# Half-sequence layout, larger moved pieces, loads issued from GpSimd and a check in tiles of its own, in a gated linear attention with a Switch expert layer

## The chip, the cores and the metric

The kernel runs on one core of a Trainium2 chip. The metric is the device time of one execution in microseconds (us); lower is better. Engines are named as in the profile: PE (matrix products), DVE (vector engine), ACT (activation functions), POOL (GpSimd), SP (the sync engine, which issues DMAs). L363 is line 363 of the kernel.

## The reference

Attention has 4 batches of 8 heads, 768 positions and 48 elements a head; the expert layer has 8 experts of 1,024 hidden elements, one for each token.

```python
mag = np.sqrt(a_re * a_re + a_im * a_im)
scale = np.minimum(mag, 0.999) / (mag + 1e-06)
a_re_n, a_im_n = (a_re * scale, a_im * scale)
for t in range(S):
    ar, ai = (a_re_n[:, :, t, :, None], a_im_n[:, :, t, :, None])
    new_re = ar * S_re - ai * S_im
    new_im = ar * S_im + ai * S_re
    kv = np.einsum('bhd,bhe->bhde', k[:, :, t], v[:, :, t])
    S_re, S_im = (new_re + kv, new_im)
    y[:, :, t] = np.einsum('bhd,bhde->bhe', q[:, :, t], S_re)
...
# x = y as (3072, 384)
logits = x @ w_gate
expert_idx = np.argmax(logits, axis=1)
# probs = softmax of logits, gate_w = probs of the chosen expert
for e in range(E):
    xe = x[expert_idx == e]
    out[expert_idx == e] = gate_w[...] * (np.maximum(xe @ w1[e], 0.0) @ w2[e])
```

## The kernel before

The recurrence is rewritten: the products of the gates up to a position become a sum of logarithms and a sum of angles, queries and keys are scaled and rotated by them, and what is left is a causal linear attention in chunks of 128 positions with a state carried between chunks.

**Units and the front.** The 3,072 positions are cut into ten units: 128, 256 and 384 positions of batch 0, two of 384 in batches 1 and 2, then 384, 256 and 128 in batch 3. `front(u)` loads a unit's gates into tile `AB` and its queries and keys into `Z` (`ld`, L280, on SP's queue; 128 partitions, two arrays, three groups of heads G, up to TU = 384 positions in fp32). ACT takes Ln and Exp, POOL multiplies `im` by the inverse, DVE works through L291 (square, whose largest value goes to `chk`), L295, L299 and the three scans of L301 (sum of logarithms), then a product of the keys, the scans of L312 (sum of angles) and L317 to L320 (whole turns off), ACT takes sine and cosine, and four products on DVE (in line 170, a helper that all products share) write the rotated keys and queries to `zp`. There are two tiles each of `AB`, `Z` and `C`, and one each of `D`, `cs` and `zp`.

**Moves.** In `zp` 128 partitions hold head elements in three groups; PE wants each head's real and imaginary parts in 96 partitions. Ten DMAs per unit (L333), five blocks for each of the two parts, move `zp` to a slot of `hz`, from SBUF to SBUF. The blocks hold three, two or one heads. Both tiles are stored by 128 positions, so that the longest piece that one DMA descriptor moves is 3 heads x 128 positions x 4 bytes = 1,536 bytes.

**Chunks.** `chunk(b, c)` works through 128 positions on PE: it turns the keys (L363, copied by ACT, L365), takes scores of four heads into a bank (L370), which DVE masks into `am` (line 170, `am<-bank,causal`), multiplies the carried state (L382) and the masked scores (L389) with queries and values, brings the state forward (L397), and turns the result into rows of tokens with the logits of the experts (L405; L411 sums the logits). `load_v` (L342) loads values by half sequences into three tiles. `route` finds each token's expert and place, and POOL scatters rows to the buffer `xs_hbm`, one DMA for 128 tokens (L467). Three DMAs (L495) fill rows of the buffer that no token may reach.

**The order of the work.** Nothing above is issued as it stands in the text. Each call adds an operation to a `Plan`, with its engine, an assumed duration, its reads and writes and, for a DMA, its size. `P.order()` simulates this list, takes the best of several orders, and the kernel writes each engine's instructions in that order; the hardware keeps it on every engine and waits on semaphores. `RATE` is the assumed rate of a DMA; one clock `dma` holds for all queues together. `after=` makes an operation start after others have been issued. Loads of unit u are placed behind the moves of unit u-2:

```python
P.add("SP", 0.65, lambda: nc.sync.dma_start(o[:, :, :, sl], src[b, :, :, :, t0:t1]), (), keys, lat=1.5, kb=2 * n * 0.512, after=moved[u - 2] if u > 1 else ())
```

**The check and the experts.** After the attention a few small DVE instructions and two matmuls (L511 to L536) find whether a general path is needed; its flag, `again`, is read later and the general path, a loop at the end, is not entered on these inputs. The check's tiles come from a pool of their own, `chkp`, opened after the attention's pool has closed; then the pool of the experts is opened. A second plan orders the experts: SP loads weights `w1b` (L573) and `w2b` (L575) and rows `xr` (L576, L579); PE turns the rows (L587) and does the two products (L598, L612; L627 for the ends of two experts together); ACT and DVE apply relu and the gate (L604, L601, L567); POOL scatters to the output (L556).

Of the kernel before, what the change touches and what calls it, by code (L numbers as in the profile page):

```python
# [43 lines left out]
class Plan:  # L44
# [25 lines left out]

    XL, TBL, RATE, SLACK = 0.12, 1.3, 0.30, 0.05

# [19 lines left out]
    def run(self, prio, edges, ins, back, stick):  # L92


        ops, n = self.ops, [len(x) for x in ins]
        ready, start = [0.0] * len(ops), [0.0] * len(ops)
        cur, dma, per_kb = None, 0.0, 1 / self.RATE / 1e3
        port, other = {"DVE": 0.0, "POOL": 0.0}, {"DVE": "POOL", "POOL": "DVE"}
        free, cand = {o["eng"]: 0.0 for o in ops}, {o["eng"]: [] for o in ops}
        for o in ops:  # L100
            if n[o["i"]] == 0:
                cand[o["eng"]].append(o["i"])
        for _ in ops:
            pick = None
            for eng, cs in cand.items():
                if not cs:
                    continue
                f = free[eng]
                fp = max(f, port[other[eng]]) if eng in port else f
                at = [max(fp if ops[i]["port"] else f, ready[i]) for i in cs]  # L110
                low = min(at)
                if pick is not None and low >= pick[2]:
                    continue
                best = None
                for i, t in zip(cs, at):
# [41 lines left out]
def gateloop_then_moe(ctx, tc, gates, qk, v, wg, w1, w2, out):  # L157
# [57 lines left out]
    with ExitStack() as att:  # L215
# [44 lines left out]
        moved = {}  # L260

        def front(u):
            b, t0, t1 = UNITS[u]
# [60 lines left out]
            for part, key, tr in ((1, Sk, si), (0, ("co",), co)):  # L324
                for x, xk, src in ((1, K, kk), (0, Q, qq)):
                    P.add("DVE", dve2(n), lambda part=part, tr=tr, x=x, src=src: tt(
                        zp[:, part, 0:nch, x].rearrange("p c g t -> p g c t"), src.rearrange("p g (c t) -> p g c t", t=128),
                        tr.rearrange("p g (c t) -> p g c t", t=128), ALU.mult), (xk,) + tuple(key), (("zp", part, x),), port=True)
            for part in (1, 0):
                for p0, p1, g0, g1, h0, d0 in BLOCKS:  # L330
                    m, r0 = g1 - g0, part * D + d0
                    eng, dma = ("ACT", nc.scalar) if u == 0 and part == 0 and h0 else ("SP", nc.sync)
                    i = P.add(eng, 0.65, lambda dma=dma, p0=p0, p1=p1, g0=g0, g1=g1, h0=h0, r0=r0, m=m, part=part: dma.dma_start(  # L333
                        hz[slot][r0:r0 + p1 - p0, cl:cl + nch, :, h0:h0 + m].rearrange("p c x h t -> p (c x) h t"),
                        zp[p0:p1, part, 0:nch, :, g0:g1].rearrange("p c x g t -> p (c x) g t")),
                        (("zp", part, 0), ("zp", part, 1)), tuple(("h", slot, cl + x, h, part, d0) for x in range(nch) for h in range(h0, h0 + m)),
                        lat=1.6, kb=2 * (p1 - p0) * m * T * 4 / 1e3)
                    moved.setdefault(u, []).append(i)

        def load_v(b, half):  # L340
            i = 2 * b + half
            P.add("SP", 0.08, lambda: nc.sync.dma_start(  # L342
                vb[i % 3], v[b, 3 * half:3 * half + 3].rearrange("c p f -> p c f")), (), (("v", i % 3),), lat=1.9, kb=590, after=moved.get(2 * b + half - 1, ()))

        def chunk(b, c):
            i = 2 * b + c // 3
# [5 lines left out]

            hq, hk = hz[slot][:, cl, 0], hz[slot][:, cl, 1]

# [132 lines left out]
        with tc.manual_schedule():  # L487
            for u in range(NU):
# [4 lines left out]
                if u == 3:  # L493
                    for h in range(3):
                        P.add("SP", 0.65, lambda h=h: nc.sync.dma_start(  # L495
                            xs_hbm.rearrange("(e s) w -> s e w", e=E)[MINC + 64 * h:MINC + 64 * h + 64],
                            bc(empty[0:64, None, :], [64, E, W])), (), (("empty", h),), lat=2, kb=E * 64 * W * 4 / 1e3, after=moved[1])
                for c in range(t0 // 128, t1 // 128):
                    chunk(b, c)
                    for r0, r1 in ROUTES[b]:  # L500
# [10 lines left out]
    again = consts.tile([1, 1], I32, name="again")  # L511
    with ExitStack() as fs:
        fp = fs.enter_context(tc.tile_pool(name="chkp", bufs=1, reuse_waits="tile"))
        ok = fp.tile([128, 4], FP32, name="ok")
        f1 = fp.tile([128, NU], FP32, name="f1")
        nc.vector.tensor_scalar(out=f1, in0=chk, scalar1=2.25, scalar2=None, op0=ALU.is_le)
        nc.vector.tensor_reduce(ok[:, 0:1], f1, axis=AX, op=ALU.min)
        lv = lend.rearrange("p b g c -> p (b g) c")
        f2 = fp.tile([128, B * G, C], FP32, name="f2")
        tt(f2, lv[:, :, 1:], lv[:, :, :C], ALU.subtract)  # L520
        nc.vector.tensor_scalar(out=f2, in0=f2, scalar1=-60.0, scalar2=None, op0=ALU.is_ge)
        nc.vector.tensor_reduce(ok[:, 1:2], f2.rearrange("p a c -> p (a c)"), axis=AX, op=ALU.min)
        f3 = fp.tile([128, B * G], FP32, name="f3")
        nc.vector.tensor_scalar(out=f3, in0=lv[:, :, C], scalar1=-100.0, scalar2=None, op0=ALU.is_ge)
        nc.vector.tensor_reduce(ok[:, 2:3], f3, axis=AX, op=ALU.min)
        nc.tensor.matmul(bank[7][:, 0:E], lhsT=ones_b, rhs=cumb, start=True, stop=True)
        f4 = fp.tile([128, E], FP32, name="f4")
        nc.vector.tensor_scalar(out=f4, in0=bank[7][:, 0:E], scalar1=float(CAP), scalar2=None, op0=ALU.is_le)
        f5 = fp.tile([128, E], FP32, name="f5")
        nc.vector.tensor_scalar(out=f5, in0=bank[7][:, 0:E], scalar1=float(MINC), scalar2=None, op0=ALU.is_ge)  # L530
        tt(f4, f4, f5, ALU.mult)
        nc.vector.tensor_reduce(ok[:, 3:4], f4, axis=AX, op=ALU.min)
        okm = fp.tile([128, 1], FP32, name="okm")
        nc.vector.tensor_reduce(okm, ok, axis=AX, op=ALU.min)
        nc.tensor.matmul(bank[7][0:1, 64:65], lhsT=okm, rhs=one, start=True, stop=True)
        nc.vector.tensor_scalar(out=again, in0=bank[7][0:1, 64:65], scalar1=127.5, scalar2=None, op0=ALU.is_lt)  # L536

# [108 lines left out]
    with tc.If(flag[0] > 0, preferred_fallthrough_block=False), ExitStack() as fs:  # L646
# [5 lines left out]
        x_tok = x_gen.rearrange("(b s) (h e) -> s h b e", b=B, h=H)  # L652
        with tc.For_i(0, S, TB) as i0:
            a = fp.tile([128, 2, B, G, TB], FP32, name="fa")
            z_ = fp.tile([128, 2, B, G, TB], FP32, name="fqk")
            for o, src in ((a, gates), (z_, qk)):
                for u in range(2):
                    for b in range(B):
                        nc.sync.dma_start(o[:, u, b], src[b, :, u, :, ds(i0, TB)])
            M_ = B * G * TB  # L660
# [93 lines left out]
def _layout(name, a):  # L754
    import numpy as _np
    if name in ('q', 'k', 'a_re', 'a_im'):
        z = _np.zeros((B, 128, G, S), a.dtype)
        for p0, p1, g0, g1, h0, d0 in BLOCKS:
            z[:, p0:p1, g0:g1] = a[:, h0:h0 + g1 - g0, :, d0:d0 + p1 - p0].transpose(0, 3, 1, 2)
        a = z  # L760
    elif name == 'v':
# [32 lines left out]
```

## Time and profile before

| | us |
|---|---|
| Median of 3 runs | 620.59 (618.48 to 620.89) |
| Profiled execution | 618.8 |
| Its span | 617.0 |
| First matmul of a unit on PE (L363) | 26.44 |
| End of the check (start of L536) | 297.69 |
| First product of the experts (L598) | 310.40 |

The mean granted clock of PE over the span was 0.889. In the profile's lines a group of instructions is written as line, engine, operation, output and input tiles, shape and count; then busy time and the mean duration of one in ns; then the idle time of the engine before them and what ended it. In the view of waits a line says which engine, at which line, waited for what, for how many us in total, how many times, and the longest. "SPq" is a queue's issuing engine. The time of a DMA in the timeline is that of its issue and not that of its transfer.

### The profile page before, as it was taken

Reading aid. Unit: us, or ns where it says so; the run is one execution under the profiler, and the core shown is the slowest. Engines: PE = TensorE matmul, PEld = TensorE weight load, DVE = VectorE, ACT = ScalarE, POOL = GpSimd, SP = SyncE. Lnnn points to the kernel's source line nnn. Section 1 sums busy time; section 2 is a strip of 40 time slices with the busy share of each in tenths; the row PEclk is TensorE's granted clock in tenths of the full one; section 3 lists DMA queues with packets and bytes.
Section 4 is the critical chain, followed back from the end, with each engine's and each line's share of the span. In section 5 each row is a group of like instructions: output and inputs, shape, how many; then the busy total and the mean of one; then the engine's idle time right before and its main releaser. Section 6 shows DMA issues by size and latency. Waiting matters only on the chain. (4 is left out here: it accounts for less than half of the span.)

```text
span 617.0 us, 7130 instructions
## 1 busy us (share of the span) xinstructions
PE 520.4 (84%) x2785; PEld 361.0 (59%) x2785; DVE 261.0 (42%) x460; ACT 207.6 (34%) x287; POOL 104.3 (17%) x112
## 2 busy tenths in 40 slices
PE   0269179976979695999199999999999999999996
PEld 0259169865868695988155555555555555555553
DVE  4957955995865954884212021111111111111111
ACT  6665755873847464774011000110001100011000
POOL 5113022303411214233200011100101011100011
PEclk9999655975957668799589999999999999999999
DMA  6584597758797948263795041630425301310000
GB/s 193 159 217 161 107 238 131 216 106 203 181 284 169 174 129 202 55 147 111 268 406 195 13 163 49 242 109 13 167 93 196 109 25 65 115 56 1 13 35 31
DMA packets 47080, 85.57 MB, mean 139 GB/s; under 512 B 3760, under 2 KB 42704, under 8 KB 44992
## 3 DMA queue, kind: packets, MB, share of 16 engines
q1 hardware_dynamic: 43424, 75.33, 44.2%
q0 software_dynamic: 3328, 9.47, 4.3%
q8 instruction: 24, 0.39, 0.3%
q10 hardware_dynamic: 288, 0.25, 0.2%
q14 instruction: 16, 0.13, 0.1%
HBM read 54.32 MB, written 12.62 MB: 109 GB/s over the span
## 5 line engine op out<-in xcount | busy, mean ns | idle before, releaser
L598 PE MATMUL bank<-xrt,w1b 128*128 128x448 f32 x384 | 148.4, 542 | 0.0
L612 PE MATMUL bank<-w2b,ht 128*128 128x384 f32 x384 | 127.5, 488 | 0.0
L598 PEld LDWEIGHTS bank<-xrt,w1b 128*128 128x128 f32 x384 | 73.3, 192 | 68.4 <-issue 64.7
L612 PEld LDWEIGHTS bank<-w2b,ht 128*128 128x128 f32 x384 | 72.5, 190 | 50.5 <-issue 4.1
L370 PE MATMUL bank<-hz 96*128 96x128 f32 x384 | 71.7, 352 | 32.9 <-DMA hz<-zp 31.6
L370 PEld LDWEIGHTS bank<-hz 96*128 96x128 f32 x384 | 64.2, 255 | 39.0 <-issue 24.0
L604 ACT ACTIVATE ht<-bank 128x448 f32<-128x448 f32 x32 | 17.4, 543 | 178.6 <-PE bank L598 178.6
L556 POOL DMA_INDIRECT out_dram<-yo,xr x24 | 23.5, 980 | 283.4 <-DVE yo L567 280.9
L601 DVE TENSOR_SCALAR ht<-bank 128x448 f32<-128x448 f32 x32 | 20.0, 624 | 111.1 <-PE bank L598 104.2
L363 PE MATMUL bank<-ident,hz 96*128 96x96 f32 x160 | 26.3, 314 | 38.3 <-DMA hz<-zp 38.3
L567 DVE TENSOR_SCALAR yo<-bank,xr 128x384 f32<-128x384 f32 x24 | 14.8, 618 | 103.2 <-PE bank L612 103.2
L363 PEld LDWEIGHTS bank<-ident,hz 96*128 96x128 f32 x160 | 21.5, 186 | 41.3 <-issue 31.9
L507 ACT ACT_TABLE_LOAD x35 | 44.9, 1283 | 1.4 <-PEq L782 0.8
L170 DVE TENSOR_TENSOR am<-bank,causal 128x512 f32<-128x512 f32 x48 | 32.2, 685 | 29.3 <-PE bank L370 29.2
L170 DVE TENSOR_TENSOR zp<-Z,cs 128x1152 f32<-128x1152 f32 (+2 forms) x40 | 42.6, 1111 | 0.7 <-ACT cs L254 0.6
L170 POOL TENSOR_TENSOR Z<-Z,AB 128x1152 f32<-128x1152 f32 (+2 forms) x9 | 22.5, 2504 | 102.3 <-ACT AB L254 51.6
L397 PEld LDWEIGHTS bank<-v,kt 128*96 128x96 f32 x320 | 36.8, 202 | 3.4 <-issue 2.8
L397 PE MATMUL bank<-v,kt 128*96 128x48 f32 x320 | 38.4, 284 | 0.4 <-ACT sb L401 0.4
L170 POOL TENSOR_TENSOR AB<-AB,C 128x1152 f32<-128x1152 f32 (+2 forms) x9 | 22.0, 2446 | 98.1 <-ACT C L254 86.6
L589 ACT COPY xrt<-bank 128x384 f32<-128x384 f32 x16 | 7.6, 478 | 86.4 <-PE bank L587 86.4
L405 PE MATMUL bank<-turn,yt 128*128 128x104 f32 x192 | 33.4, 330 | 3.3 <-ACT xg L409 1.8
L389 PE MATMUL bank<-am,v 128*48 128x128 f32 x384 | 33.9, 328 | 0.0
(112 smaller groups left out, 517.1 us busy)
## 6 DMA issues: line engine op xcount, KB each, us to landing
w1b<-in_w_dram SPq DMA_DIRECT2D x8, 1536.0 KB, 7.4
w2b<-in_w_dram SPq DMA_DIRECT2D x8, 1536.0 KB, 8.5
hz<-zp SPq DMA_DIRECT2D x24, 432.0 KB, 6.7
AB<-in_gates_dram SPq DMA_DIRECT2D x6, 1152.0 KB, 6.6
Z<-in_qk_dram SPq DMA_DIRECT2D x6, 1152.0 KB, 10.5
xr<-xs_hbm SPq DMA_DIRECT2D x8, 579.0 KB, 3.8
v<-in_v_dram SPq DMA_DIRECT2D x8, 576.0 KB, 10.2
xs_hbm<-empty SPq DMA_DIRECT2D x3, 772.0 KB, 13.2
```

The lines of the kernel that those rows point to most:

```text
L170: (eng or nc.vector).tensor_tensor(out=o, in0=a, in1=b, op=op)
L363: nc.tensor.transpose(KT[hf][:, (h % 4) * 96:(h % 4) * 96 + 96], hk[:, h], ident[0:96, 0:96])
L370: nc.tensor.matmul(SC[hf][:, (h % 4) * 128:(h % 4) * 128 + 128], lhsT=hk[:, h], rhs=hq[:, h], start=True, stop=True)
L389: nc.tensor.matmul(YT[ps, (h // 2) * 128:(h // 2) * 128 + 128], lhsT=V[:, cl, h * D:h * D + D], rhs=am[2 * par + hf][:, h % 4, :], start=( ...
L397: nc.tensor.matmul(ST[0:96, h * D:h * D + D], lhsT=kt[par][:, h * 96:h * 96 + 96], rhs=V[:, cl, h * D:h * D + D], start=(c == 0 and h == 0 ...
L405: nc.tensor.matmul(XT[:, p * 104:p * 104 + 104], lhsT=yt[par][:, p * 128:p * 128 + 128], rhs=turn[:, p, :], start=True, stop=True)
L507: nc.scalar.preload_act_table_set("natural_log_exp_and_others" if P.cur == "LE" else "trig_and_small")
L556: i = nc.gpsimd.indirect_dma_start(out=out[:, :], out_offset=bass.IndirectOffsetOnAxis(ap=index, axis=0), in_=y, in_offset=None, bounds_ch ...
L598: nc.tensor.matmul(HB[hb][:, 0:CAP], lhsT=w1b[ws][:, c:c + 128], rhs=xrt[s][:, d, :], start=(d == 0), stop=(d == DT - 1))
L601: M.add("DVE", 0.6, lambda f_=f_, hb=hb: nc.vector.tensor_scalar_max(ht[s][:, f_, :], HB[hb][:, 0:CAP], 0.0), (("H", hb),), (("ht", s, f_),))
L604: M.add("ACT", 0.6, lambda f_=f_, hb=hb: nc.scalar.activation(ht[s][:, f_, :], HB[hb][:, 0:CAP], func=ACT.Relu), (("H", hb),), (("ht", s, ...
L612: nc.tensor.matmul(OB[ob][:, 0:DM], lhsT=ht[s][:, f_, j * 128:j * 128 + 128], rhs=w2b[ws][:, f_ * DM:f_ * DM + DM], start=(f_ == 0), stop= ...
```

## The change

- Gates and the pair of queries and keys are stored by half sequences, (4, 2, 128, 2, 3, 384) instead of (4, 128, 2, 3, 768), so a unit of 384 positions is one run of 9,216 bytes in each partition.
- `zp` and `hz` become flat. A full unit writes them by kind (key or query), head and position, so that a moved piece is 3 x 384 x 4 = 4,608 bytes (3,072 and 1,536 for blocks of two heads and one). The four shorter units keep the old arrangement; `operand` gives PE the right view.
- The loads of gates, queries and keys, values, and the three fills of empty rows are issued by POOL instead of SP, and the loads no longer have `after=` the moves.
- The planner assumes 0.22 instead of 0.30 for the rate, and keeps a DMA clock for each issuing engine.
- The check's tiles come from the pool of constants.
- The loop of the general path, which is not entered, reads the new layout.

```diff
-    XL, TBL, RATE, SLACK = 0.12, 1.3, 0.30, 0.05
+    XL, TBL, RATE, SLACK = 0.12, 1.3, 0.22, 0.05
...
-        cur, dma, per_kb = None, 0.0, 1 / self.RATE / 1e3
+        cur, dma, per_kb = None, {}, 1 / self.RATE / 1e3
...
-                dma = end = max(dma, end) + o["kb"] * per_kb
+                dma[eng] = end = max(dma.get(eng, 0.0), end) + o["kb"] * per_kb
...
-        zp, = buf("zp", 1, [128, 2, TU // 128, 2, G, 128])
+        zp, = buf("zp", 1, [128, 2, 2 * G * TU])
...
-        hz = buf("hz", 2, [96, TU // 128, 2, H, 128])
+        hz = buf("hz", 2, [96, 2 * H * TU])
...
+        def operand(t, full, z, c):
+
+            if full:
+                return t.rearrange("p (z h t) -> p z h t", z=2, h=H)[:, z, :, c * 128:c * 128 + 128]
+            return t.rearrange("p (c z h t) -> p c z h t", z=2, h=H, t=128)[:, c, z]
...
-                P.add("SP", 0.65, lambda: nc.sync.dma_start(o[:, :, :, sl], src[b, :, :, :, t0:t1]), (), keys, lat=1.5, kb=2 * n * 0.512, after=moved[u - 2] if u > 1 else ())
+                P.add("POOL", 1.1, lambda: nc.gpsimd.dma_start(
+                    o[:, :, :, sl], src[b, t0 // TU, :, :, :, t0 % TU:t0 % TU + T]), (), keys, lat=1.9, kb=2 * n * 0.512)
...
+                        if T == TU:
+                            tt(zp[:, part].rearrange("p (z g t) -> p z g t", z=2, g=G)[:, x], src, tr, ALU.mult)
+                        else:
+                            o = zp[:, part].rearrange("p (c z g t) -> p z g c t", z=2, g=G, t=128)[:, x, :, 0:nch]
+                            tt(o, src.rearrange("p g (c t) -> p g c t", t=128), tr.rearrange("p g (c t) -> p g c t", t=128), ALU.mult)
...
+                        if T == TU:
+                            o, i = o.rearrange("p (z x) -> p z x", z=2), i.rearrange("p (z x) -> p z x", z=2)
+                            dma.dma_start(o[:, :, h0 * T:(h0 + m) * T], i[:, :, g0 * T:g1 * T])
...
-            P.add("SP", 0.08, lambda: nc.sync.dma_start(
-                vb[i % 3], v[b, 3 * half:3 * half + 3].rearrange("c p f -> p c f")), (), (("v", i % 3),), lat=1.9, kb=590, after=moved.get(2 * b + half - 1, ()))
...
+            P.add("POOL", 1.1, lambda: nc.gpsimd.dma_start(
+                vb[i % 3], v[b, 3 * half:3 * half + 3].rearrange("c p f -> p c f")), (), (("v", i % 3),), lat=1.9, kb=590)
...
-            hq, hk = hz[slot][:, cl, 0], hz[slot][:, cl, 1]
+            hq, hk = (operand(hz[slot], full, z, cl) for z in range(2))
...
-                        P.add("SP", 0.65, lambda h=h: nc.sync.dma_start(
+                        P.add("POOL", 1.1, lambda h=h: nc.gpsimd.dma_start(
...
-    with ExitStack() as fs:
-        fp = fs.enter_context(tc.tile_pool(name="chkp", bufs=1, reuse_waits="tile"))
-        ok = fp.tile([128, 4], FP32, name="ok")
+    ok = consts.tile([128, 4], FP32, name="ok")
...
```

The order that the planner writes changes with the costs, on DVE, ACT and PE too. On SP only the moves and one small load of the gate weights are left before the experts. On POOL the loads stand between the products.

More of the change, by code (lines that the diff above doesn't have):

```diff
@@ L325, in front, with f @@
                 for x, xk, src in ((1, K, kk), (0, Q, qq)):
-                    P.add("DVE", dve2(n), lambda part=part, tr=tr, x=x, src=src: tt(
-                        zp[:, part, 0:nch, x].rearrange("p c g t -> p g c t"), src.rearrange("p g (c t) -> p g c t", t=128),
-                        tr.rearrange("p g (c t) -> p g c t", t=128), ALU.mult), (xk,) + tuple(key), (("zp", part, x),), port=True)
+                    def f(part=part, tr=tr, x=x, src=src):
+                        if T == TU:
[3 more added lines that the diff above has]
+                            tt(o, src.rearrange("p g (c t) -> p g c t", t=128), tr.rearrange("p g (c t) -> p g c t", t=128), ALU.mult)
+                    P.add("DVE", dve2(n), f, (xk,) + tuple(key), (("zp", part, x),), port=True)
             for part in (1, 0):
@@ L332, in front, with f @@
                     eng, dma = ("ACT", nc.scalar) if u == 0 and part == 0 and h0 else ("SP", nc.sync)
-                    i = P.add(eng, 0.65, lambda dma=dma, p0=p0, p1=p1, g0=g0, g1=g1, h0=h0, r0=r0, m=m, part=part: dma.dma_start(
-                        hz[slot][r0:r0 + p1 - p0, cl:cl + nch, :, h0:h0 + m].rearrange("p c x h t -> p (c x) h t"),
-                        zp[p0:p1, part, 0:nch, :, g0:g1].rearrange("p c x g t -> p (c x) g t")),
+                    def f(dma=dma, p0=p0, p1=p1, g0=g0, g1=g1, h0=h0, r0=r0, m=m, part=part):
+                        o, i = hz[slot][r0:r0 + p1 - p0], zp[p0:p1, part]
+                        if T == TU:
+                            o, i = o.rearrange("p (z x) -> p z x", z=2), i.rearrange("p (z x) -> p z x", z=2)
+                            dma.dma_start(o[:, :, h0 * T:(h0 + m) * T], i[:, :, g0 * T:g1 * T])
+                        else:
+                            o = o.rearrange("p (c x) -> p c x", x=H * 128)[:, 2 * cl:2 * (cl + nch), h0 * 128:(h0 + m) * 128]
+                            dma.dma_start(o, i.rearrange("p (c x) -> p c x", x=G * 128)[:, 0:2 * nch, g0 * 128:g1 * 128])
+                    i = P.add(eng, 0.65, f,
                         (("zp", part, 0), ("zp", part, 1)), tuple(("h", slot, cl + x, h, part, d0) for x in range(nch) for h in range(h0, h0 + m)),
@@ L341, in load_v, with chunk @@
             i = 2 * b + half
-            P.add("SP", 0.08, lambda: nc.sync.dma_start(
-                vb[i % 3], v[b, 3 * half:3 * half + 3].rearrange("c p f -> p c f")), (), (("v", i % 3),), lat=1.9, kb=590, after=moved.get(2 * b + half - 1, ()))
-        def chunk(b, c):
+            P.add("POOL", 1.1, lambda: nc.gpsimd.dma_start(
+                vb[i % 3], v[b, 3 * half:3 * half + 3].rearrange("c p f -> p c f")), (), (("v", i % 3),), lat=1.9, kb=590)
+        def chunk(b, c, full):
             i = 2 * b + c // 3
@@ L498, in gateloop_then_moe @@
                 for c in range(t0 // 128, t1 // 128):
-                    chunk(b, c)
+                    chunk(b, c, t1 - t0 == TU)
                     for r0, r1 in ROUTES[b]:
@@ L511, in gateloop_then_moe @@
     again = consts.tile([1, 1], I32, name="again")
-    with ExitStack() as fs:
-        fp = fs.enter_context(tc.tile_pool(name="chkp", bufs=1, reuse_waits="tile"))
-        ok = fp.tile([128, 4], FP32, name="ok")
[L515 to L536, printed above, removed]
@@ new lines, in gateloop_then_moe @@
+    ok = consts.tile([128, 4], FP32, name="ok")
+    f1 = consts.tile([128, NU], FP32, name="f1")
+    nc.vector.tensor_scalar(out=f1, in0=chk, scalar1=2.25, scalar2=None, op0=ALU.is_le)
+    nc.vector.tensor_reduce(ok[:, 0:1], f1, axis=AX, op=ALU.min)
+    lv = lend.rearrange("p b g c -> p (b g) c")
+    f2 = consts.tile([128, B * G, C], FP32, name="f2")
+    tt(f2, lv[:, :, 1:], lv[:, :, :C], ALU.subtract)
+    nc.vector.tensor_scalar(out=f2, in0=f2, scalar1=-60.0, scalar2=None, op0=ALU.is_ge)
@@ new lines, in gateloop_then_moe @@
+    nc.vector.tensor_reduce(ok[:, 1:2], f2.rearrange("p a c -> p (a c)"), axis=AX, op=ALU.min)
+    f3 = consts.tile([128, B * G], FP32, name="f3")
+    nc.vector.tensor_scalar(out=f3, in0=lv[:, :, C], scalar1=-100.0, scalar2=None, op0=ALU.is_ge)
+    nc.vector.tensor_reduce(ok[:, 2:3], f3, axis=AX, op=ALU.min)
+    nc.tensor.matmul(bank[7][:, 0:E], lhsT=ones_b, rhs=cumb, start=True, stop=True)
+    f4 = consts.tile([128, E], FP32, name="f4")
+    nc.vector.tensor_scalar(out=f4, in0=bank[7][:, 0:E], scalar1=float(CAP), scalar2=None, op0=ALU.is_le)
@@ new lines, in gateloop_then_moe @@
+    f5 = consts.tile([128, E], FP32, name="f5")
+    nc.vector.tensor_scalar(out=f5, in0=bank[7][:, 0:E], scalar1=float(MINC), scalar2=None, op0=ALU.is_ge)
+    tt(f4, f4, f5, ALU.mult)
+    nc.vector.tensor_reduce(ok[:, 3:4], f4, axis=AX, op=ALU.min)
+    okm = consts.tile([128, 1], FP32, name="okm")
+    nc.vector.tensor_reduce(okm, ok, axis=AX, op=ALU.min)
+    nc.tensor.matmul(bank[7][0:1, 64:65], lhsT=okm, rhs=one, start=True, stop=True)
+    nc.vector.tensor_scalar(out=again, in0=bank[7][0:1, 64:65], scalar1=127.5, scalar2=None, op0=ALU.is_lt)
@@ L652, in gateloop_then_moe @@
         x_tok = x_gen.rearrange("(b s) (h e) -> s h b e", b=B, h=H)
-        with tc.For_i(0, S, TB) as i0:
+        with tc.For_i(0, S // TU) as hi, tc.For_i(0, TU, TB) as j0:
+            i0 = hi * TU + j0
             a = fp.tile([128, 2, B, G, TB], FP32, name="fa")
@@ L658, in gateloop_then_moe @@
                     for b in range(B):
-                        nc.sync.dma_start(o[:, u, b], src[b, :, u, :, ds(i0, TB)])
+                        nc.sync.dma_start(o[:, u, b], src[b].rearrange("s p u g t -> p s u g t")[:, ds(hi, 1), u, :, ds(j0, TB)])
             M_ = B * G * TB
@@ L759, in _layout @@
             z[:, p0:p1, g0:g1] = a[:, h0:h0 + g1 - g0, :, d0:d0 + p1 - p0].transpose(0, 3, 1, 2)
-        a = z
+        a = z.reshape(B, 128, G, S // TU, TU).transpose(0, 3, 1, 2, 4)
     elif name == 'v':
@@ L785 @@
         a = [_layout(x, _np.asarray(inputs[x])) for x in of]
-        a = _np.ascontiguousarray(_np.stack(a, axis=2)) if len(a) == 2 else a[0]
+        a = _np.ascontiguousarray(_np.stack(a, axis=3)) if len(a) == 2 else a[0]
         arrays[f"in_{name}_dram"] = a
```

## The prediction

> **What bounds the kernel now.** I read the page first, then the waits, stretches of the span one by one, and the timeline where PE stands still.
>
> ```profile
> span 617.0 us, 7130 instructions
> PE 520.4 (84%) x2785; PEld 361.0 (59%) x2785; DVE 261.0 (42%) x460; ACT 207.6 (34%) x287; POOL 104.3 (17%) x112
> PEclk9999655975957668799589999999999999999999
> ```
>
> PE is busy for 84% of the span, but not of one kind. The granted clock (tenths, 15.4 us a slice) falls to 5 to 7 in slices 5 to 18, the attention stage, and is full after that. Two stretches of the windows view show the rest (length; busy us of PE, PEld, DVE, ACT, POOL with instructions; clock; DMA share; GB/s):
>
> ```profile
> 135.00:150.00 15.00, 7.42 (x42) 6.50 (x42) 12.84 (x23) 5.04 (x8) 2.75 (x1) 0.50 1.04 216
> 315.00:400.00 85.00, 85.00 (x272) 45.79 (x271) 12.96 (x25) 6.87 (x13) 6.86 (x7) 1.00 0.44 162
> ```
>
> From about 310 us the experts run with PE full at clock 1.00; nothing in the change shortens an expert matmul, so that half is a fixed 300 us. Before it, a unit of 384 positions alternates: PE stands, then works at clock 0.50. What it stands for is in the waits (total us, times, longest):
>
> ```profile
> PE bank L363 <- DMA hz<-zp: 38.3, 6, 26.4
> PE bank L370 <- DMA hz<-zp: 31.6, 9, 14.9
> DVE am L170 <- PE bank L370: 29.2, 16, 7.8
> ...
> SPq L333 <- DVE zp L170: 122.1, 11, 22.5
> ...
> SPq L573 <- PE bank L535: 15.3, 1, 15.3
> ```
>
> It is a ring: PE waits for moved heads (26.4 of the 38.3 is the start), the moves wait on SP for zp from DVE, and DVE waits in its fixed order for PE's scores before it may go on with the next unit's front. The moves of successive full units begin at 67.2, 94.5, 128.9, 160, 197.7, 227.7 and 261.2 us: 32.3 us a unit. DVE's own work for one unit, summed from its rows, is 27.2 us (front head L291, L295, L299 and three L301 scans 6.9; L312 3.0; L317, L318, L320 3.4; key product 1.35; four zp 5.4; six am 4.1; logits and routing about 3). PE's is 22.9 us at full clock. So 27.2 is DVE's floor, and 5.1 us of every unit are waiting.
>
> **Sum, against the profiled execution** (618.8 us, span 617.0, 1.8 around it; the median of the runs is 620.6, also 1.8 above it).
>
> *Loads from SP to GpSimd.* 20 loads of gates and queries, 8 of values and 3 empties leave SP's queue. SP stood 122 us waiting for zp, so its freed time (0.6 to 1.9 us each) is worth nothing; what hides it is that wait. On POOL the nearest row is the scatter:
>
> ```profile
> L467 POOL DMA_INDIRECT xs_hbm<-xg,slot x24 | 25.3, 1052 | 19.2 <-DVE cum L170 8.3 <-issue 5.2 <-DVE ohs L425 2.4
> ```
>
> 0.98 us and 0.30 to the next: 1.28 each, 40 us on an engine that is 17% busy, in gaps where POOL waits 86.6 us for ACT's C and 51.6 for ACT's AB. That is free except at the start. In the new order POOL does its memsets (to 3.8 us), the first gates, nine copies (3.3), then six more issues before u1's product, which ran at 10.14. At 1.28: 3.8 + 3.3 + 7 x 1.28 = 16.1, 6 later; unit 0's gates are issued 2.5 later (3.8 for 1.26). PE's first chunk hangs on the second number, the next unit on the first: bounds +2.5 and +6, I take +3. The other end goes by pieces: a scatter has 128, as has a full unit's load now (9,216 B a partition), but the loads of units 0 and 1 have 768, so 5.9 us each, and those of values 384. The seven issues count as 5.5 of 5.9: 3.8 + 3.3 + 32.5 = 39.6, +29. I take the row as it stands, since one issue is one instruction there too, and keep +29 for a rival.
>
> POOL's queue also gets waits: gates wait for the tile's last product, queries for zp of two units before, values for PE's use of three units before. Behind each stands a later unit's product, for which DVE's L291 waits. The nearest row is the same wait on SP:
>
> ```profile
> SPq L342 <- PE bank L389: 17.1, 3, 11.4
> ```
>
> Bounds 0 and +17; I take 0, since those products are for units two ahead in the new order, one unit (32 us) before DVE asks for them. If the lead is lost, the 11.4 is the price of one.
>
> *Larger load pieces.* Loads in pieces of 1,536 B ran at 372 GB/s (below), expert weights at 300 to 315 us, a row of 12 KB a piece, at 383: 3% of some 6 us, hidden a unit ahead. 0.
>
> *Larger moved pieces* (4,608 B instead of 1,536). Moves alone, and loads alone, at the same piece size:
>
> ```profile
> 134.00:138.00 4.00, 2.87 (x18) 2.64 (x16) 3.96 (x6) 0.47 (x2) 0.00 (x0) 0.50 0.94 165
> 146.00:150.00 4.00, 4.00 (x24) 3.77 (x25) 2.09 (x5) 1.44 (x3) 0.00 (x0) 0.50 1.06 372
> ```
>
> At 1,536 B a load gets 372, a move 165. Piece size is not what parts them, so I expect 0; the bound is the load's rate: a unit's 2.36 MB in 6.4 instead of 14.3 us, -7.9 a unit. The Trainium skill, "DMA: Bandwidth & Descriptors", section "Why small descriptors are slow (HBM only)", says transfers inside SBUF don't suffer from small pieces; by it this term is 0, by a price on each piece up to -7.9, and the two rows lie on the page's side.
>
> *Loads beside moves.* The loads of unit u+2 no longer wait behind the moves of u, so 2.9 MB may run in the same time. The trace has 1.2 MB of scatters there (first row alone, then two units with them):
>
> ```profile
> 128.00:146.00 18.00, 7.79 (x55) 6.44 (x51) 17.76 (x25) 9.36 (x13) 2.75 (x1) 0.60 0.89 152
> 160.00:177.00 17.00, 12.25 (x130) 10.93 (x129) 15.55 (x21) 8.21 (x13) 3.83 (x4) 0.87 0.92 202
> 227.70:247.00 19.30, 12.81 (x136) 11.62 (x135) 10.62 (x21) 9.89 (x15) 8.93 (x9) 0.84 0.84 184
> ```
>
> -1.0 to +1.3 us for 1.2 MB; by bytes -2.4 to +3.1 a unit. I take +1 in five units, +5. The same page, section "Issuing engines are not separate DMA queues", speaks against the change: all issuers share the sixteen engines and only issue time is saved. By it the 2.9 MB would cost 2.9 MB / 372 GB/s = 7.8 us a unit; the rows above show the total rate rise from 152 to 184 and 202 instead.
>
> *Order.* The planner gets other costs (RATE, one clock for each issuer). DVE now runs L291 of unit u+2 straight behind zp of u, and the masks am between the four zp pieces:
>
> ```profile
> 69.61 1.35 DVE L170 TENSOR_TENSOR zp<-Z,cs 128x1152 f32<-128x1152 f32 x1
> ...
> 90.84 1.16 ACT L254 ACTIVATE AB<-AB 128x1152 f32<-128x1152 f32 x1
> ...
> 102.47 1.35 DVE L291 CUSTOM_DVE_ANT_0 C<-AB 128x1152 f32<-128x1152 f32 x1
> ```
>
> Before, zp of unit 2 ended at 70.96, the first Ln of unit 4 came 20 us later, L291 31 us later. The 6.9 us of front head then fill waits for am. The price: the last zp piece stands behind an am of the previous unit's second chunk, so a late PE holds the moves. Stepping units 3 to 6 through the new order with these durations, moves landing 12 us after zp, gives unit ends 8.6, 7.5, 12 and 16 us earlier. I take -16 and let the +5 stand against it. Bounds: 0 and 6 x -5.1 = -31 (DVE never waits).
>
> *Check in its own tiles.* SP reached the first expert weights at 282.4 and stood 15.3 us for the last check matmul, since the tiles came from the pool reused there.
>
> ```profile
> 297.72 0.36 SPq L573 DMA_DIRECT2D w1b<-in_w_dram  x1
> 300.11 0.38 SPq L576 DMA_DIRECT2D xr<-xs_hbm  x1
> ...
> 306.76 3.84 PE L587 MATMUL bank<-ident,xr 128*128 128x128 f32 x15 [9.11 <-DMA xr<-xs_hbm]
> ```
>
> The weights now go early; xr still waits for the last scatter at 300.11, but alone on the engines: its usual 3.8 us for 6.65, -2.9 (bounds 0 and -2.9). The check's own instructions stay, under the wait for xr.
>
> Sum: +3 + 0 + 0 + 5 - 16 - 2.9 = -10.9, so 607.9 by the profiled run and 609.7 by the median. I say 610.
>
> **Rivals.**
> *DVE's floor.* PE never runs dry, its clock stays up and units follow at 27.2 us: -31 + 3 - 2.9, or 590. For it: 22.9 us of PE work fits. Against: the moves land 12 us after zp, and a gap of 2 to 3 us already halved the clock.
> *Slower: GpSimd's issue is priced by pieces.* The start is +29, the rest -13.9: 636. It decides from about 3.1 us an issue of 768 pieces, where 5.5 of them give back the gain (5.5 x 3.1 + 7.1 - 10.1 = 14). For it: nothing in the trace issues 768 pieces from POOL. Against: the scatter's fixed 0.98.
> *Loads slow the moves.* +3.1 in six units, and PE waits for all of it: +19 + 3 - 16 - 2.9, or 624. It decides when moves land after PE has finished the unit before, as they did in every wait above.
> *It does not do what it says:* the moves' 12 us and the half clock set the cycle whatever DVE's order, -2.9 + 3: 621.
>
> **Chances.** Forecast 0.42 (own range 597 to 617); DVE's floor 0.13; issue by pieces 0.25; loads slow the moves 0.12; nothing 0.08. 0.5% is 3.1 us, about what a measurement can tell here. Faster: 0.42 + 0.13 = 0.55. Same: 0.08 and half of the 624 case, 0.15 rounded up. Slower: the rest, 0.30. For 8 in 10 I leave out half of the floor case below and half of the issue case above: 589 to 637.
>
> **What would show it.** Right: loads issued from POOL at about 1.3 us each; moves near 165 GB/s with 4,608 B pieces; L291 of unit 4 some 20 us sooner than 102 us; units 29 to 30 us apart; w1b issued before 290, and L587 about 4 us after xr. Wrong: moves well over 200 GB/s alone (piece size counted: faster than 600), POOL rows of several us at the start and PE's first chunk after 35 us (the issue rival), or PE waits on hz over 70 us with clock 0.5 in as many slices as before.

## The result, and the profile after

The changed kernel takes 639.54 us (median of 4 runs, 636.57 to 642.51) where the kernel before takes 619.54: the ratio is 1.0329, with a 95% interval of 1.0261 to 1.0396. The prediction was 610, with a range of 589 to 637. The profiled execution took 636.57 us, its span was 634.9. Ratios and times below leave disturbed executions out; where only two were left, no interval is given.

The head of the page and the view of waits of the changed kernel:

```profile
span 634.9 us, 7136 instructions
PE 522.9 (82%) x2785; PEld 359.8 (57%) x2785; DVE 262.9 (41%) x460; ACT 203.0 (32%) x283; POOL 127.6 (20%) x143
PEclk9995555579776878769859999999999999999998
```

```profile
PE bank L388 <- DMA hz<-zp: 68.6, 8, 35.2
...
DVE am L170 <- PE bank L388: 50.6, 24, 7.5
```

PE's work is what it was (522.9 for 520.4 us). Its waits for moved heads need care, since the first and longest of them stood at L363 before and stands at the scores (L388, formerly L370) now. These are the second line of the changed kernel, and then the one line of e1 below, which has all of the change but the new queue:

```profile
PE bank L381 <- DMA hz<-zp: 4.0, 4, 1.9
```

```profile
PE bank L388 <- DMA hz<-zp: 39.9, 7, 24.2
```

Both lines together are 69.9 us before (38.3 and 31.6, with 26.4 for the first wait) and 72.6 us after (68.6 and 4.0, with 35.2 for the first). So against the kernel before only the first wait grew, by 8.8 us; the later ones fell from 43.5 to 37.4 us, since the change also brings a new order (with it alone, in e4, they are 17.1). Against e1 all of them grew: the first from 24.2 to 35.2, the later ones from 15.7 to 37.4.

DVE's waits for scores went from 29.2 to 50.6 us. The clock is at half speed in slices 4 to 8 of 40, and its mean over the span is 0.866 where it was 0.889. The experts hardly changed: from the issue of the first xr to the end it is 315.7 us here (319.16 to 634.9) and 316.9 before (300.11 to 617.0). The whole loss lies in the attention stage, 8.8 us of it ahead of PE's first matmul. From there to the first xr PE stands still for 67 us, where before it was 58 (windows view, first before, then after):

```profile
26.00:300.00 274.00, 215.51 (x1793) 194.89 (x1793) 197.26 (x339) 166.48 (x219) 69.00 (x48) 0.77 0.70 169
```

```profile
35.00:319.00 284.00, 217.00 (x1793) 193.57 (x1793) 195.67 (x336) 157.36 (x211) 81.86 (x68) 0.73 0.61 155
```

Unit 2 shows how. This is the timeline of the changed kernel (start, duration of the issue, what; in brackets the idle time before it):

```profile
78.53 12.90 SPq L349 DMA_DIRECT2D hz<-zp  x10
...
86.01 0.56 POOL L286 DMA_DIRECT2D AB<-in_gates_dram  x1 [0.30 <-POOL Z L170]
...
87.27 0.76 POOL L360 DMA_DIRECT2D v<-in_v_dram  x1 [0.70 <-PE bank L407]
...
88.02 0.98 POOL L286 DMA_DIRECT2D Z<-in_qk_dram  x1
...
96.78 1.65 PE L388 MATMUL bank<-hz 96*128 96x128 f32 x6 [7.10 <-DMA hz<-zp]
...
105.27 0.98 PE L388 MATMUL bank<-hz 96*128 96x128 f32 x3 [1.91 <-DMA hz<-zp]
```

SP issues the second half of the moves at 86.96, when the last zp is done. Between 86.0 and 88.0 tiles come free for POOL too (that of the queries by the same last zp), and 2.9 MB of loads go out beside them. In the view of DMAs for 86 to 90 us (queue, kind: packets, MB, share of the sixteen engines), POOL's queue is the only one with packets:

```profile
q0 software_dynamic: 80, 0.74, 66.0%
```

From the end of the last zp (86.9) it is 18 us until PE waits for the last time for this unit's heads (105.27); before it was 12 (71.0 to 83.17). What the loads brought was the queries of unit 4, the gates of unit 5 and values, which nothing waited for yet.

### The profile page after: what moved, and what is told of

The parts are those of the page before. It is cut to its first block, busy times and chain, and to the rows that moved or that the text cites. A ratio compares the mean times of both kernels' runs of the same rounds, so it can differ in the third digit from the quotient of the medians.

```text
span 634.9 us, 7136 instructions
## 1 busy us (share of the span) xinstructions
PE 522.9 (82%) x2785; PEld 359.8 (57%) x2785; DVE 262.9 (41%) x460; ACT 203.0 (32%) x283; POOL 127.6 (20%) x143
## 5 line engine op out<-in xcount | busy, mean ns | idle before, releaser
L388 PE MATMUL bank<-hz 96*128 96x128 f32 x384 | 71.5, 348 | 73.1 <-DMA hz<-zp 68.6
L388 PEld LDWEIGHTS bank<-hz 96*128 96x128 f32 x384 | 63.6, 252 | 78.6 <-DMA hz<-zp 66.2
L620 ACT ACTIVATE ht<-bank 128x448 f32<-128x448 f32 x32 | 17.4, 543 | 178.3 <-PE bank L614 178.3
L170 DVE TENSOR_TENSOR am<-bank,causal 128x512 f32<-128x512 f32 x48 | 32.7, 685 | 50.6 <-PE bank L388 50.6
L170 DVE TENSOR_TENSOR zp<-Z,cs 128x1152 f32<-128x1152 f32 (+2 forms) x40 | 44.6, 1152 | 3.5 <-ACT cs L254 3.2
L407 PE MATMUL bank<-am,v 128*48 128x128 f32 x384 | 36.8, 336 | 1.4 <-DVE am L170 1.4
L485 POOL DMA_INDIRECT xs_hbm<-xg,slot x24 | 28.6, 1193 | 42.5 <-issue 32.1
L423 PE MATMUL bank<-turn,yt 128*128 128x104 f32 x192 | 33.3, 328 | 1.9 <-ACT yt L411 1.4
L383 ACT COPY kt<-bank 128x384 f32<-128x384 f32 x40 | 18.2, 477 | 49.3 <-PE bank L381 49.2
```

The source lines that it names most:

```text
L170: (eng or nc.vector).tensor_tensor(out=o, in0=a, in1=b, op=op)
L388: nc.tensor.matmul(SC[hf][:, (h % 4) * 128:(h % 4) * 128 + 128], lhsT=hk[:, h], rhs=hq[:, h], start=True, stop=True)
L407: nc.tensor.matmul(YT[ps, (h // 2) * 128:(h // 2) * 128 + 128], lhsT=V[:, cl, h * D:h * D + D], rhs=am[2 * par + hf][:, h % 4, :], start=( ...
L423: nc.tensor.matmul(XT[:, p * 104:p * 104 + 104], lhsT=yt[par][:, p * 128:p * 128 + 128], rhs=turn[:, p, :], start=True, stop=True)
L485: i = nc.gpsimd.indirect_dma_start(out=xs_hbm[:, :], out_offset=bass.IndirectOffsetOnAxis(ap=R[slot][:, c:c + 1], axis=0), in_=xg[:, (g0 + ...
```

## The experiments

The runs were taken on several chips, on which the kernel before takes 619.5 to 627.7 us; so their ratios to it are compared, and not their times.

**Theories.** 1: loads on a queue of their own run at the same time as the moves, which PE waits for, and delay them. 2: the planner's new order costs (masks between the zp pieces). 3: the larger moved pieces move worse. Rivals to the first inside POOL: what stands behind POOL's waits, its later start, or turns that the queues take piece by piece.

**e1: loads back on SP, all else as changed.**

```diff
-                P.add("POOL", 1.1, lambda: nc.gpsimd.dma_start(
+                P.add("SP", 0.65, lambda: nc.sync.dma_start(
...
+                    ..., lat=1.5, kb=2 * n * 0.512, after=moved[u - 2] if u > 1 else ())
```

(and so for values and empty rows)

> The changed kernel with its loads of gates, queries, values and the empty rows back on SP's queue and behind the moves, as before; layout, larger moved pieces, planner rate and check tiles stay changed. Theory 1 (loads on a queue of their own take the DMA engines while PE waits for moves): the 20 us come back, 610 to 621 us, moves land within 13 us again. Theory 2 (the planner's new order, masks between the zp pieces): little comes back, 632 us or more. Theory 3 (the larger moved pieces move worse): 632 us or more. If only the later start counts: about 630.

Measured: 0.984 of the kernel before (0.976 to 0.993), so about 30 us faster than the changed kernel. Theories 2 and 3 fall as the main cause: both parts are still in it.

**e2: only the loads moved to POOL, in the kernel before.**

```diff
-                P.add("SP", 0.65, lambda: nc.sync.dma_start(o[:, :, :, sl], ...
+                P.add("SP", 0.65, lambda: nc.gpsimd.dma_start(o[:, :, :, sl], ...
```

(and so for values and empty rows)

> The kernel before with one edit: the same loads are issued by POOL instead of SP, in the planner's old order; old storage, old pieces (1,536 bytes), old check pool. Theory 1: slower than before by 8 to 25 us, with moves that land later wherever a load runs beside them. Theories 2 and 3: within 4 us of before, apart from a start that is 3 to 9 us later.

Measured: 1.093 (1.085 to 1.101), 57 us slower, more than twice what theory 1 expected. In its profile PE waits 115.4 us for moved heads (69.4 at L363, 46.0 at L370). The rest of the change wins some of it back. Why the same loads cost twice as much in the old order as in the new one (e9) was not tried.

**e3: old moved pieces in the changed kernel.**

```diff
-                        if T == TU:
+                        if False:
...
-                    chunk(b, c, t1 - t0 == TU)
+                    chunk(b, c, False)
```

> The changed kernel with zp and hz stored by 128 positions again for all units, so that moved pieces are 1,536 bytes; all else as changed. Theory 3 (larger pieces move worse): 620 to 630 us. Theory 1: 637 us or more, since smaller pieces get a smaller share beside loads in pieces of 9,216 bytes. If pieces count for nothing: within 3 us of the changed kernel.

Measured: 1.043 (1.034 to 1.053) where the changed kernel has 1.033 (1.026 to 1.040). Theory 3 falls: the larger pieces help if anything.

**e4: only the planner's costs, in the kernel before.**

```diff
-    XL, TBL, RATE, SLACK = 0.12, 1.3, 0.30, 0.05
+    XL, TBL, RATE, SLACK = 0.12, 1.3, 0.22, 0.05
...
-        cur, dma, per_kb = None, 0.0, 1 / self.RATE / 1e3
+        cur, dma, per_kb = None, {}, 1 / self.RATE / 1e3
```

> The kernel before with the planner's rate 0.22 and a DMA clock for each issuer, nothing else; the orders on DVE, ACT, PE and SP change. Theory 2 (the order is what costs): 630 to 640 us. Theories 1 and 3: within 5 us of before; the prediction's order gain would show as up to 11 us faster.

Measured: 0.987 (0.983 to 0.991), 8 us faster. The order is a gain. Its clock row and its wait for scores, from the page and the waits of e4:

```profile
PEclk9999999788769785988589999999999999999999
```

```profile
DVE am L170 <- PE bank L370: 18.7, 15, 2.8
```

The 29.2 us of waits for scores became 18.7, and the clock falls to half in two slices, where it was five.

**e5: loads on POOL, but not before the moves have landed.**

```diff
+                P.add("POOL", 0.1, lambda: nc.gpsimd.tensor_copy(
+                    gate, operand(hz[us], ut1 - ut0 == TU, 0, uc)[:, :, 0]), <keys of the moves of u - 2>, (("gate", u),))
```

> The changed kernel, loads still issued by POOL, but before the two loads of unit u POOL copies 8 elements in each of 96 rows out of the moved heads of unit u-2, so that it waits until those moves have landed. Theory 1 (loads and moves at the same time on the DMA engines): most of the 30 us that the loads cost comes back but for the start, 615 to 630 us on a chip where the kernel before takes 620; units follow with scores within 3 us of the last move. Rival (POOL's queue itself: products and scatters stand behind loads that wait): more waits on POOL, 635 us or more.

Measured: 1.028 (1.022 to 1.034), which is 637 us on a chip where the kernel before takes 620. The expectation failed and the time is in the range of the rival, but the run does not answer its question alone (e9 and e12 do): the planner knows the copy and writes other orders, POOL now waits 54.8 us for moves, and values and empty rows were not held back. These collide in their turn. From 175 to 184 us the view of DMAs of e5 has POOL's queue with empty rows and values, while the second half of unit 5's moves was being issued on SP from 174.62:

```profile
q0 software_dynamic: 463, 1.95, 92.6%
q1 hardware_dynamic: 129, 0.18, 7.3%
```

The five moves of that half took 13.85 us to issue, where all ten of a unit take 11 to 12 in e1, and PE waited 8.82 us for that unit.

**e6: the four first loads on SP, the rest on POOL.**

```diff
+                if u < 2:
+                    P.add("SP", 0.65, lambda: nc.sync.dma_start(
```

> The changed kernel with the four loads of gates and queries of units 0 and 1 on SP, the rest on POOL. If the start is a cost of its own, unit 1's moves begin 6 to 9 us earlier and the end comes 6 to 11 us earlier (629 to 634 where the changed kernel takes 640). If the collisions of loads and moves take it back, less than 4 us.

Measured: 645.2 us, 1.03 of the kernel before (two runs): no gain. The planner wrote other orders here as well, so it tells little of the start; unit 1's moves began at 42.3 us for 43.1.

**e7: small load pieces on POOL.** The storage of before in the changed kernel.

```diff
-                    o[:, :, :, sl], src[b, t0 // TU, :, :, :, t0 % TU:t0 % TU + T]), ...
+                    o[:, :, :, sl], src[b, :, :, :, t0:t1]), ...
```

> The changed kernel with gates and queries stored as before, so that a full unit's load from POOL is 768 pieces of 1,536 bytes instead of 128 of 9,216; moves stay at 4,608. If queues take turns piece by piece, moves get three times a load's share and the time falls, 622 to 632 us. If POOL's issue or its ring pays for each piece, it rises, 650 us or more. If only the bytes count: within 4 us of the changed kernel.

Measured: 1.034 (1.028 to 1.039), as the changed kernel. Neither turns by pieces nor a price on each piece.

**e8: pieces and check tiles alone.** e1 with the planner's costs of before.

```diff
-    XL, TBL, RATE, SLACK = 0.12, 1.3, 0.22, 0.05
+    XL, TBL, RATE, SLACK = 0.12, 1.3, 0.30, 0.05
```

> The kernel before with the half-sequence storage, the larger moved pieces and the check in the pool of constants; loads on SP behind the moves and the planner's costs as before. Prediction: pieces 0, check tiles -2.9, so 617 where before takes 620. If the larger pieces shorten a unit's moves as the changed kernel and its version with old pieces suggest (6 us for six units), 611 to 614.

Measured: 622.2 us where before took 626.1 (two runs), 0.994. The two runs are 6 us apart (619.2 and 625.2), so the 3.8 us agree with the prediction's -2.9 and do not exclude 6.

**e9 to e12: the queue alone, with the orders of PE, ACT and DVE those of e1 (but for two small casts at DVE's start in e9).** The planner goes on taking the loads for SP's; only the engine that issues is another.

```diff
e9   all loads:      nc.sync.dma_start -> nc.gpsimd.dma_start
e10  queries, keys:  (nc.gpsimd if u > 1 and src is qk else nc.sync).dma_start
e11  gates:          (nc.gpsimd if u > 1 and src is gates else nc.sync).dma_start
e12  all on SP, and after the load of queries: nc.gpsimd.tensor_copy(scr, zp[:, 0, 0:8])
```

> The version with loads on SP (e1) with every load, values and empty rows issued by POOL; the orders of PE, ACT and DVE stay those of e1, so only the queue differs. Theory 1 (loads take the DMA engines from the moves): slower than e1 by 25 to 50 us, as the changed kernel is. Rival (the changed kernel's own order on DVE and PE is what costs): within 10 us of e1.

> e1 with the loads of queries and keys of units 2 to 9 issued by POOL, nothing else. Their tile becomes free when the last zp of two units before ends, which is when that unit's moves start, so theory 1 puts 1.18 MB beside every move: 8 to 20 us slower than e1. Rival (POOL's queue is blocked): the same delay would show without any transfer in e12.

> e1 with the loads of gates of units 2 to 9 issued by POOL, nothing else. Their tile becomes free after the last product of the unit two before, some 10 us ahead of its moves, so the transfer is mostly over when they start. Theory 1: 0 to 6 us slower than e1. If any load on POOL's queue costs the same: as e10.

> e1 with loads on SP, and at each place where e10 issues a load from POOL a POOL copy of 8 columns of zp into a scratch tile, which waits for the same zp and moves nothing by DMA. Theory 1: within 4 us of e1. Rival (products and scatters wait behind POOL's waits): 8 to 20 us slower than e1, like e10.

| | of the kernel before | against e12, us |
|---|---|---|
| e12, waits without transfer | 0.982 (0.975 to 0.989) | 0 |
| e11, gates on POOL | 0.998 (0.995 to 1.002) | +10 |
| e10, queries on POOL | 1.015 (1.009 to 1.021) | +20 |
| e9, all on POOL | 1.029 (two runs) | +29 |

(1% is 6.2 us.) POOL's waits for zp cost nothing: e12 is e1 again, so the rival of the blocked queue falls for these loads; the waits of values for PE were not tried without their transfer, but in the profile of e9, with all loads on POOL, DVE waits next to nothing for POOL's products:

```profile
DVE C L298 <- POOL AB L170: 1.2, 1, 1.2
```

The transfers cost, and the whole 30 us are there with nothing changed but the queue. The same unit 2 in e1 and then in e10, from the timelines:

```profile
72.50 11.11 SPq L349 DMA_DIRECT2D hz<-zp  x10
...
83.64 1.62 PE L388 MATMUL bank<-hz 96*128 96x128 f32 x6 [6.57 <-DMA hz<-zp]
...
83.71 0.53 SPq L286 DMA_DIRECT2D AB<-in_gates_dram  x1
```

```profile
74.84 12.59 SPq L349 DMA_DIRECT2D hz<-zp  x10
...
79.19 0.57 POOL L286 DMA_DIRECT2D Z<-in_qk_dram  x1 [12.02 <-DVE zp L170]
...
92.21 1.65 PE L388 MATMUL bank<-hz 96*128 96x128 f32 x6 [13.52 <-DMA hz<-zp]
```

On one queue the loads stand behind the moves (83.71), and PE starts 11.1 us after the first move. With 1.18 MB issued from POOL at 79.19, between the two halves of the moves, it is 17.4: 6.2 us for one load. In the view of DMAs of e10 POOL's queue has the engines alone from 82 to 84 us:

```profile
q0 software_dynamic: 69, 0.64, 98.5%
```

The gates were expected at 0 to 6 and cost 10: in this order their loads for units 5, 6, 8 and 9 also went out at 103.20, 134.35, 201.19 and 233.57, while moves were being issued (98.3 to 108.8, 129.2 to 138.8, 195.5 to 207.7, 231.4 to 243.5).

**e13 to e16: another engine's queue, the remaining parts, and the base again.** All on e1.

```diff
e13  queries, keys:  (nc.scalar if u > 1 and src is qk else nc.sync).dma_start
e14  values but the first, and empty rows:  nc.gpsimd
e15  units 0 and 1 and the first values:    nc.gpsimd
e16  e1 unchanged
```

> e1 with the loads of queries and keys of units 2 to 9 issued by ACT instead of SP, at the place of the plan where e10 issues them from POOL. If two queues at the same time are what costs, whichever engine issues: 10 to 25 us slower than e1, as e10 (20). If POOL's queue alone takes the engines ahead of SP's: 0 to 6 us slower than e1, the moves landing within 13 us. ACT may also wait for zp ahead of its own work, which would show as ACT idle on the DMA line.

> e1 with the loads of values (but the first) and the three fills of empty rows on POOL. What is left of the whole (34) after queries (20) and gates (10) is 4 us, shared with the start: 0 to 6 us slower than e1, most of it in the one unit beside which 2.3 MB of empty rows are written.

> e1 with the loads of units 0 and 1 and the first values on POOL, nothing else. By the prediction's step: POOL's first load 2.5 us later and unit 1's product 6 us later, so 2.5 to 6 us slower than e1; if the start weighs as in the changed kernel (unit 1's moves 9 us later), 9.

> e1 once more, on the chip of e13 to e15, with more rounds: 0.976 to 0.993 of the kernel before, and the base that the other three are held against.

(The expectation of e14 takes 34 for the whole; by the table above it is 29.) Measured: e16 0.978 (0.973 to 0.984), e13 0.993 (0.989 to 0.997), e14 0.992 (0.987 to 0.997), e15 0.987 (0.982 to 0.992). Against e16 the queries on ACT cost 9 us, where from POOL they cost 20; values and empty rows 9, above what was expected; the first units 5, with intervals that just overlap. So a second queue costs on ACT as well, about half as much. Collisions are in it: in the profile of e13 the moves of unit 3 are issued from 100.47 to 119.63, ACT issues its load at 106.97, and from 112 to 116 us the view of DMAs has ACT's queue (q10) ahead of SP's (q1):

```profile
q10 hardware_dynamic: 100, 0.89, 75.8%
q1 hardware_dynamic: 84, 0.28, 23.0%
```

How much of the 9 us is ACT's own waiting is open. The parts on POOL (20, 10, 9, 5) sum to 44 and the whole is 29, so they do not add; delays of the same unit that overlap would explain it, which is not shown.

The version to keep is e1, 0.978 to 0.984 of the kernel before: the order, the pieces and the check tiles, without the new queue.

## Why the prediction failed, by its own steps

- **Loads beside moves** is the step that failed. It took +1 us a unit, +5 in all, with bounds of -2.4 to +3.1, from units that had 1.2 MB of scatters beside their moves. Measured: 6.2 us for 1.18 MB beside unit 2's moves, 20 us for the queries alone, and 29 for all loads, the start included. The scatters were the wrong row: POOL issues them 1.28 us apart, while a load puts 1.18 MB on the engines at once, while the moves are being issued. That this difference is the reason is our reading; no run varied it alone. The prediction's estimate by bytes, 7.8 us a unit (2.9 MB at 372 GB/s), would have given 47 us for six units: too much against 29 measured, but the right cause, with the sign against the change. The Trainium skill, "DMA: Bandwidth & Descriptors", section "Issuing engines are not separate DMA queues", says that DMAs of all issuers run on the same sixteen engines and interleave, and that several issuers only save issue time; the loss of 29 us agrees with it, while for some microseconds one queue had the engines alone (82 to 84 us in e10).
- **The rival "loads slow the moves"** named the mechanism, and was priced too low, at 624, with a chance of 0.12, from the same scatters.
- **Order**: -16 with bounds 0 and -31; alone it gave -8 (e4). Right in sign, half the size. The prediction stepped units 3 to 6 and took the gain of the last as that of the end. In e4 the moves of units 2 and 7 begin at 72.9 and 220.5 us, 29.5 us a unit, where before it was 67.2 and 227.7, 32.1 a unit; and the last unit's moves begin 14.5 us earlier (260.5 for 275.0), near the forecast. But the first rows of the experts go out only 5.4 us earlier (294.7 for 300.1): behind the last moves 34.2 us follow, where before it was 25.1. This end was in no term.
- **Start**: +3 between 2.5 and 6; alone +5.4 (e15), where unit 1's moves begin 2.8 us later than in e1 (38.49 for 35.66). In the changed kernel they began 9.2 us later than before (43.09 for 33.91), because unit 0's moves had met the first big load of queries, issued at 26.93. From 28 to 34 us the view of DMAs has that load on q0 and the moves on q10 (issued by ACT) and q1:

```profile
q0 software_dynamic: 144, 1.18, 68.1%
q10 hardware_dynamic: 284, 0.24, 15.9%
q1 hardware_dynamic: 112, 0.15, 8.6%
```

- **Issue on POOL**: 1.28 us were taken, and 5.9 by pieces was a rival. Measured for the gates of full units: 0.55 to 0.62 us in 128 pieces (the changed kernel) and 0.83 to 0.89 in 768 (e7); the longest was 1.04. Six times the pieces cost 0.3 us, and this rival is out. Unit 1's product at 16.37 us, foretold at 16.1, was right by accident: POOL had finished issuing at 11.8 and waited 4.59 us for ACT.

```profile
7.05 0.86 POOL L286 DMA_DIRECT2D AB<-in_gates_dram  x1
...
16.37 1.98 POOL L170 TENSOR_TENSOR AB<-AB,C 128x768 f32<-128x768 f32 x1 [4.59 <-ACT C L254]
```

- **Waits on POOL's queue**: 0 with a bound of +17. In the changed kernel POOL stands 39.7 us for PE ahead of loads of values, but the only wait of DVE for POOL ahead of the experts is 0.4 us at the start, so 0 holds as far as the profile shows.

```profile
POOL v L360 <- PE bank L407: 39.7, 4, 18.2
...
DVE base L200 <- POOL base_i L198: 0.4, 1, 0.4
```

- **Check tiles**: -2.9. The wait is right: the rows land 4.06 us after their issue (6.65 before; 6.9 in e4, which has the old pool, and 4.0 in e1), and the weights go out 21 us ahead of the rows. From that issue to the end, though, only 1.2 us were won (315.7 for 316.9).

```profile
298.11 0.44 SPq L589 DMA_DIRECT2D w1b<-in_w_dram  x1
...
319.16 0.39 SPq L592 DMA_DIRECT2D xr<-xs_hbm  x1
...
323.22 2.89 PE L603 MATMUL bank<-ident,xr 128*128 128x128 f32 x12 [6.64 <-DMA xr<-xs_hbm]
```

- **Pieces**: 0, nearly right. Eight microseconds of moves alone, in 1,536 bytes in the kernel before and then in 4,608 bytes in e1 (last column GB/s):

```profile
69.00:77.00 8.00, 0.00 (x0) 0.00 (x0) 7.96 (x9) 5.06 (x6) 0.00 (x0) 0.50 0.99 189
```

```profile
74.00:82.00 8.00, 3.07 (x30) 2.61 (x26) 4.84 (x5) 4.19 (x5) 0.00 (x0) 1.00 0.97 205
```

That is 8%, one microsecond of a unit's 11 to 12, far from a load's 372 GB/s (the prediction's 165 for small pieces was read from 4 us; over these 8 us it is 189). e1 and e4, which differ in pieces and check tiles, are 0.3% apart. e3 and e8 leave room for a few microseconds.

- **Signs**: L298 (formerly L291) of unit 4 came at 86.86, 15.6 us sooner than 102.47, as forecast in kind; units were 33.3 us apart (moves at 78.5 and 245.0 for units 2 and 7) and not 29 to 30. "PE's first chunk after 35 us" came true (35.18) although the rival that it was to show is out, and "over 70 us" of waits on hz came true (72.6) where the kernel before had 69.9, so it told little. The clock was not full from slice 19 on, as the prediction reads it: slices 20 and 21 are at 5 and 8 tenths.

With the measured terms the sum comes out near: 618.8 - 8 (order) - 2.6 (check) + 29 (loads, start included) = 637.2, or 638.6 with 1.2 for the check, where the profiled execution took 636.6. Of the 28.7 us that separate it from 607.9, loads and start are 21 (8 taken, 29 measured) and the order 8. The terms come from different chips and from one order of work, and e2 shows that they depend on it, so part of this agreement is luck.

## What to carry to other kernels

Before a transfer is moved to a free queue, ask which transfer it used to stand behind: here the old queue's order let the moves that PE waited for go before loads that were needed a unit later, and the stall of SP that looked like waste was that priority. A transfer released by the same event as an urgent one will collide with it, however late its result is needed: in e10 all six loads of queries issued by the zp of a full unit went out while that unit's moves were being issued. When a change has several parts, take a price for contention from a row with the same burst at the same moment, not from one with the same bytes.

## What the runs showed of the hardware that was not expected

- Between two queues the sixteen engines were not shared evenly: in e5 POOL's queue moved 1.95 MB in 9 us while SP's moved 0.18 MB with moves waiting, and five moves took 13.85 us to issue. In the changed kernel (86 to 90 us) and in e10 (82 to 84 us) POOL's queue was the only one with packets. ACT's queue against SP's had 75.8% to 23.0% (e13).
- The size of the loads' pieces did not change the time of the whole (e7 1.034, the changed kernel 1.033), and six times the pieces made an issue on POOL only 0.3 us longer (0.83 to 0.89 us for 0.55 to 0.62).
- The mean granted clock did not tell the time of an execution. In the profile of e4 the same 2,785 matmuls were busy for 515.5 us instead of 520.4, with a mean clock of 0.928 instead of 0.889; but on the chip of e13 to e16 the kernel before took 626.8 and 627.0 us at mean clocks of 0.927 and 0.929, and 623.2 to 630.6 us at 0.880 to 0.891. So the higher clock is not shown to be a gain of its own.
